# Choosing the engine of copies, squares, products and remainders step by step, with a fixed issue order, in a linear-attention and mixture kernel

## The chip, the core and the metric

The kernel runs on one core of one Trainium2 chip. The metric is the device time of one execution in microseconds (us). Three runs of the kernel before took 484.88, 486.04 and 486.46 us; the median is 486.04 us. About 0.3% (1.5 us) is what a comparison of this kernel can tell from no change.

## The reference, cut to what matters

```python
def _attn_ref(q, k, v, f_logit):          # q, k, v, f_logit: (4, 8, 768, 48)
    f = 1.0 / (1.0 + np.exp(-f_logit))
    state = np.zeros((B, H, D, D), dtype=np.float32)
    for t in range(S):
        state = f[:, :, t, :, None] * state + np.einsum('bhd,bhe->bhde', k[:, :, t], v[:, :, t])
        y[:, :, t] = np.einsum('bhd,bhde->bhe', q[:, :, t], state)
    return y

def _moe_ref(x, w_in, w_out):             # x: (3072, 384), w_in: (384, 2048), w_out: (2048, 384)
    h = x @ w_in
    sp = np.where(h > 20.0, h, np.log1p(np.exp(np.minimum(h, 20.0))))
    g = h * np.tanh(sp)
    return g @ w_out
```

The attention's output, put in rows of 384, is the x of the second part. All is float32 in and out.

## The kernel before

**Attention.** The 768 tokens are cut into 24 chunks of 128 tokens (4 batches by 6 pieces; n counts them, n = 0 to 23). For each chunk, `prep(n)` floors the log gates (`L529`), takes exponent and logarithm (`L532`, `L533`), sums them (by a matmul for the first four chunks, by the scan `L542` for the rest), takes two exponents (`L548`), multiplies k and q by them (`times`, `L411`) and keeps the decay at the chunk's end (`L555`). `attn0` to `attn3` turn k over, make the scores and mask them (`L589`), copy the turned k (`L612`), update the state (`L688` to `L693`, and the product with the decay, `L780`) and make the output. The output is evicted from PSUM whole by `L789` for the first four chunks (into `spareh`), and as a rounded part and a remainder after that (`L808` and `L809`, into `xt`).

**Second part.** The tokens form six groups of 512, and the 2048 inner columns form 16 tiles of 128, j = 0 to 15. A unit u is one group and one tile (98 units; the first four are half a group wide). Its input product h is at `L317` (nine matmuls of 512 columns in float32r, three products that make up for the rounding) or, for the first seven units, at `L327` (plain float32). Then g = h tanh(softplus(h)) is made in `mish`: exponent `L351` on ScalarE, clamp and add `L352` on VectorE, square (`L343` on ScalarE for u < 24, `L344` on VectorE after that), logarithm `L354` and exponent `L355` on ScalarE, product `L356` on VectorE, which is the last to read h. `L358` rounds g to gh on ScalarE, and the remainder g - gh goes to gl: on VectorE for u < 24 (`L347`), on GpSimd after that (`L348`). The output product of a unit is at `L365` (`L330` for the first seven), two units after the input product. There are two PSUM banks for h, so the input product of unit u + 2 waits until `L356` of unit u has read h.

**Weights.** Each weight tile j comes as 64-bit words and is put together by `load_w`: `L476` on ScalarE, then `L478`, `L479` and `L481` on VectorE. `split_w` rounds the tile on ScalarE (`L493`) and takes the remainder on VectorE (`L494`). `split_x` does the same to the first group's x (`L502`, `L503`). All 16 tiles are prepared once, while the first two groups run, and stay in SBUF.

**Order.** The kernel doesn't issue what it computes at once. Every step goes to a `Plan` (`add`) with its engine, a cost, and what it reads and writes; 1813 steps in all. `Plan.order` of the kernel before packs them by rank, forwards and backwards, tries random shifts from a list of seeds, and keeps the best; each engine's queue is then in that order. Steps marked `port` are packed as if VectorE and GpSimd could not run them at the same time. Where TensorE has nothing planned, `Plan.issue` puts in filler matmuls on zeros (`idle`, `L462`) until the first output product. An example of the planned costs, and the line that they belong to:

```python
def T_DVE(n):
    return n / 0.96 + 72
add("dve", T_DVE(W_TILE), lambda: nc.vector.scalar_tensor_tensor(   # W_TILE = 768; line L479
```

Of the kernel before, what the change touches and what calls it, by code (L numbers as in the profile page):

```python
# [10 lines left out]
F32 = mybir.dt.float32  # L11
# [35 lines left out]
SETTING = (600.0, 20.0)  # L47
MOVES = (
# [25 lines left out]
COLD = 1000.0  # L74


class Plan:
# [8 lines left out]
    def __init__(self):  # L86
        self.steps = []
        self.writer, self.readers = {}, {}
        self.glued = {}

# [13 lines left out]

    def glue(self, n):
        self.glued[len(self.steps)] = len(self.steps) - n

    def pack(self, rank, ahead, haste, back=False):


        steps = self.steps
# [4 lines left out]
        for i in range(count):  # L116
            for b in before[i]:
                after[b].append(i)
# [1005 lines left out]
```

## Time and profile before

| what | value |
|---|---|
| three runs, median (lowest to highest) | 486.04 us (484.88 to 486.46) |
| the profiled execution | 484.71 us |
| its span, first to last instruction | 482.9 us |
| TensorE (PE) busy | 464.4 us, 96% |
| weight loads (PEld) busy | 391.2 us, 81% |
| ScalarE (ACT) busy | 352.8 us, 73% |
| VectorE (DVE) busy | 343.8 us, 71% |
| GpSimd (POOL) busy | 144.3 us, 30% |

The profiled execution's own time is 1.8 us over its span. The table's shares are means over stages that differ: VectorE is near 100% from about 45 to 140 us and at 50% near the end, while GpSimd does nothing between 80 and 140 us.

### The profile page before, as it was taken

Reading aid. Unit: us, or ns where it says so; the run is one execution under the profiler, and the core shown is the slowest. Engines: PE = TensorE matmul, PEld = TensorE weight load, DVE = VectorE, ACT = ScalarE, POOL = GpSimd, SP = SyncE. Lnnn points to the kernel's source line nnn. Section 1 sums busy time; section 2 is a strip of 40 time slices with the busy share of each in tenths; the row PEclk is TensorE's granted clock in tenths of the full one; section 3 lists DMA queues with packets and bytes.
Section 4 is the critical chain, followed back from the end, with each engine's and each line's share of the span. In section 5 each row is a group of like instructions: output and inputs, shape, how many; then the busy total and the mean of one; then the engine's idle time right before and its main releaser. Section 6 shows DMA issues by size and latency. Waiting matters only on the chain.

```text
span 482.9 us, 12157 instructions
## 1 busy us (share of the span) xinstructions
PE 464.4 (96%) x5032; PEld 391.2 (81%) x5032; DVE 343.8 (71%) x600; ACT 352.8 (73%) x662; POOL 144.3 (30%) x126
## 2 busy tenths in 40 slices
PE   8988989899999999999999999999999999999994
PEld 8766547787778888888888888888888888888883
DVE  4579999999996878777676766865875554554551
ACT  6779887999989677667777787677676466665650
POOL 0411120000013354343543443343333233342431
PEclk9999999999999999999999999999999999999998
DMA  7776656453402253421211240220230000010001
GB/s 246 226 252 222 222 183 220 140 178 118 160 36 89 93 188 106 154 70 63 89 50 73 88 139 16 90 88 33 90 110 1 3 12 23 1 65 0 1 0 71
DMA packets 17102, 48.42 MB, mean 100 GB/s; under 512 B 2000, under 2 KB 2000, under 8 KB 17040
## 3 DMA queue, kind: packets, MB, share of 16 engines
q1 hardware_dynamic: 17040, 47.59, 28.9%
q8 instruction: 40, 0.66, 0.5%
q14 instruction: 22, 0.18, 0.1%
HBM read 39.32 MB, written 6.29 MB: 94 GB/s over the span
## 4 chain that ended last, share of the span: by engine, by line
PE 71%; DVE 13%; ACT 12%; issue 3%; DVEq 0%; ACTq 0%
PE o L365 30%; PE h L317 30%; DVE wt L479 2%; PE at L755 2%; DVE ng L356 2%; ACT ng L354 2%; PE at L762 1%; ACT ng L355 1%; ACT ng L343 1%; DVE wl L494 1%; PE at L609 1%; DVE gl L347 1%; ACT wt L476 1%; PE o L462 1%; PE h L582 1%
## 5 line engine op out<-in xcount | busy, mean ns | idle before, releaser
L317 PE MATMUL h<-xt,wh 128*128 128x512 f32 x546 | 164.2, 382 | 3.7 <-DVE ng L356 3.7
L348 POOL TENSOR_TENSOR gl<-ng,gh 128x512 fp32r<-128x512 f32 x74 | 100.6, 1362 | 174.4 <-ACT gh L358 153.4
L317 PEld LDWEIGHTS h<-xt,wh 128*128 128x128 f32 x546 | 101.6, 189 | 21.3 <-DVE ng L356 7.0
L356 DVE SCALAR_TENSOR_TENSOR ng<-ng,h 128x512 f32<-128x512 f32 x91 | 62.1, 684 | 63.6 <-ACT ng L355 63.0
L365 PE MATMUL o<-gh,wh 128*128 128x512 f32 x273 | 106.3, 389 | 0.0
L365 PE MATMUL o<-gl,wh 128*128 128x512 f32 x273 | 103.6, 379 | 0.5 <-DVE gl L347 0.5
L317 PE MATMUL h<-xt,wl 128*128 128x512 f32 x273 | 103.5, 379 | 0.0
L365 PE MATMUL o<-gh,wl 128*128 128x512 f32 x273 | 103.5, 379 | 0.0
L354 ACT ACTIVATE ng<-ng 128x512 f32<-128x512 f32 (+1 forms) x98 | 60.7, 620 | 35.3 <-DVE ng L344 31.1
L351 ACT ACTIVATE ng<-h 128x512 f32<-128x512 f32 (+1 forms) x98 | 57.3, 585 | 31.9 <-PE h L317 30.9
L358 ACT ACTIVATE gh<-ng 128x512 fp32r<-128x512 f32 x91 | 56.6, 625 | 22.3 <-PE o L365 14.6
L352 DVE TENSOR_SCALAR ng<-ng 128x512 f32<-128x512 f32 (+1 forms) x98 | 47.9, 489 | 30.0 <-ACT ng L351 29.5
L355 ACT ACTIVATE ng<-ng 128x512 f32<-128x512 f32 (+1 forms) x98 | 60.6, 619 | 2.4
L411 POOL TENSOR_TENSOR in<-in,inv 128x512 f32<-128x512 f32 x20 | 24.9, 1244 | 119.6 <-ACT inv L548 119.5
L365 PEld LDWEIGHTS o<-gl,wh 128*128 128x128 f32 x273 | 51.6, 189 | 8.2 <-DVE gl L347 0.9
L365 PEld LDWEIGHTS o<-gh,wh 128*128 128x128 f32 x273 | 51.6, 189 | 7.9 <-issue 0.2
L317 PEld LDWEIGHTS h<-xt,wl 128*128 128x128 f32 x273 | 51.6, 189 | 7.3
L365 PEld LDWEIGHTS o<-gh,wl 128*128 128x128 f32 x273 | 51.6, 189 | 6.8 <-issue 0.2
L344 DVE TENSOR_TENSOR ng<-ng 128x512 f32<-128x512 f32 x74 | 54.7, 739 | 2.2
L542 DVE TENSOR_TENSOR_SCAN inv<-gate,state 128x516 f32<-128x516 f32 x20 | 24.6, 1228 | 2.3 <-ACT gate L533 2.1
L780 POOL TENSOR_TENSOR state<-tmp,ends 128x192 f32<-128x192 f32 x20 | 14.7, 735 | 19.0 <-PE at L755 7.9
L479 DVE SCALAR_TENSOR_TENSOR wt<-raw,wt 128x768 int32<-128x768 int32 x16 | 17.9, 1119 | 0.2
(147 smaller groups left out, 571.7 us busy)
## 6 DMA issues: line engine op xcount, KB each, us to landing
in<-lk SPq DMA_DIRECT2D x18, 512.0 KB, 4.4
raw<-ww SPq DMA_DIRECT2D x12, 768.0 KB, 4.2
in<-qv SPq DMA_DIRECT2D x18, 512.0 KB, 4.2
out<-ob SPq DMA_DIRECT2D x18, 256.0 KB, 2.1
raw<-ww SPq DMA_DIRECT2D x8, 384.0 KB, 4.4
in<-lk SPq DMA_DIRECT2D x8, 256.0 KB, 3.6
in<-qv SPq DMA_DIRECT2D x8, 256.0 KB, 4.2
xt<-xt SPq DMA_DIRECT2D x15, 128.0 KB, 3.0
```

The source lines that it names most:

```text
L317: nc.tensor.matmul(h, w[:, a * P : (a + 1) * P], read(xt[:, x, a], part), start=(n == 0), stop=(n == 3 * NK - 1))
L344: ("dve", T_DVE(w), 1, lambda: nc.vector.tensor_tensor(n, n, n, ALU.mult))
L348: ("pool", T_POOL(w), 1, lambda: nc.gpsimd.tensor_tensor(gl, g, gh.bitcast(F32), ALU.subtract))
L351: ("act", T_ACT(w, True), 0, lambda: nc.scalar.activation(n_out, h, AF.Exp)),
L352: ("dve", T_DVE(w / 2), 1, lambda: nc.vector.tensor_scalar(n, n, E_CAP, 1.0, ALU.min, ALU.add)),
L354: ("act", T_ACT(w), 0, lambda: nc.scalar.activation(g, n, AF.Ln, bias=0.5, scale=0.5)),
L355: ("act", T_ACT(w), 0, lambda: nc.scalar.activation(g, g, AF.Exp, scale=-1.0)),
L356: ("dve", T_DVE(w), 0, lambda: nc.vector.scalar_tensor_tensor(g_out, g_in, 1.0, h, ALU.subtract, ALU.mult)),
L358: ("act", T_ACT(w), 0, lambda: nc.scalar.activation(gh, g, AF.Copy)),
L365: nc.tensor.matmul(o, w, read_again(x), start=(first and i == 0), stop=(last and i == 2))
L411: add("pool" if on_pool else "dve", cost, lambda: eng.tensor_tensor(dst, x, y, ALU.mult), reads, writes, port=port)
L479: add("dve", T_DVE(W_TILE), lambda: nc.vector.scalar_tensor_tensor(t, low, 29, t, ALU.logical_shift_right, ALU.bitwise_or), [kr], [kt], po ...
```

## The change

The planner's search is gone. The order of the 1813 steps is a table, `ORDER`, and a string, `CHOICES`, picks the engine of each step that can run on more than one (`Plan.either`). Nothing is computed otherwise than before: the steps, and what each waits for, are the same 1813, and 195 of them change their engine.

```diff
-SETTING = (600.0, 20.0)
-MOVES = (
-    100004, 100007, 100010, 100011, 100013, 100015, 100017, 100019, 100023, 100030, 100031, 100033, 100036,
+ORDER = (
+    0, 1, 35, 60, 110, 36, 85, 61, 175, 86, 11, 2, 12, 3, 13, 4, 14, 5, 15, 17, 6, 7, 8, 16, 9, 19, 18, 24, 10, 37,
+CHOICES = (
+    "1000010101000000001000100110000111000010000001001000000010000100010000100100100000000001001001100110"
...
+    def either(self, options, reads, writes):
+
+        n = len(self.open)
+        self.open.append((len(self.steps), options))
+        engine, cost, port, issue = options[int(CHOICES[n]) if n < len(CHOICES) else 0]
+        self.add(engine, cost, issue, reads, writes, port=port)
...
+        square = prefer(
+            ("act", T_ACT(w), 0, lambda: nc.scalar.activation(n, n, AF.Square)),
+            ("dve", T_DVE(w), 1, lambda: nc.vector.tensor_tensor(n, n, n, ALU.mult)),
+            False,
         )
+        high = prefer(
+            ("act", T_ACT(w), 0, lambda: nc.scalar.activation(gh, g, AF.Copy)),
+            ("dve", T_DVE(w / 2), 1, lambda: nc.vector.tensor_copy(gh, g)),
+            not early,
+        ) + (("pool", w * 1.1 + 75, 1, lambda: nc.gpsimd.tensor_copy(gh, g)),)
+        low = prefer(
+            ("dve", T_DVE(w), 1, lambda: nc.vector.tensor_tensor(gl, g, gh.bitcast(F32), ALU.subtract)),
+            ("pool", T_POOL(w), 1, lambda: nc.gpsimd.tensor_tensor(gl, g, gh.bitcast(F32), ALU.subtract)),
+            not early,
         )
...
+        def copy(cols, dst, src, reads, writes):
+
+            plan.either((
+                ("act", T_ACT(cols, True), 0, lambda: nc.scalar.activation(dst, src, AF.Copy)),
+                ("dve", T_DVE(cols), 0, lambda: nc.vector.tensor_copy(dst, src)),
+            ), reads, writes)
...
-            add("act", T_ACT(W_TILE) + 65, lambda: nc.scalar.activation(
+            add("act", T_ACT(W_TILE) + 80 + 320 * late, lambda: nc.scalar.activation(
                 t.bitcast(F32), high.bitcast(F32), AF.Copy, scale=2.0**-112), [kr], [kt])
...
-            add("dve", T_DVE(W_TILE), lambda: nc.vector.scalar_tensor_tensor(
+            add("dve", T_DVE(W_TILE) + 220 * late, lambda: nc.vector.scalar_tensor_tensor(
                 t, low, 29, t, ALU.logical_shift_right, ALU.bitwise_or), [kr], [kt], port=True)
...
-                add("dve", T_DVE(w / 2), lambda s=s: nc.vector.tensor_scalar(
+                clamp = nc.gpsimd if n >= 5 * GC else nc.vector
+                add("pool" if n >= 5 * GC else "dve", w * 1.1 + 75 if n >= 5 * GC else T_DVE(w / 2), lambda s=s, clamp=clamp: clamp.tensor_scalar(
                     f[:, s], f[:, s], L_CAP, None, ALU.max), (), kf, port=True)
...
-            add("act", T_ACT(GT, True), lambda: nc.scalar.activation(kt_s, b, AF.Copy), [key], ["kt"])
+            copy(GT, kt_s, b, [key], ["kt"])
...
-                    add("pool", T_POOL(NP * D), lambda: nc.gpsimd.tensor_tensor(sv, tv, dv, ALU.mult),
-                        pairs(("end", n)) + [ktmp], [("st", batch)])
+                    plan.either((
+                        ("pool", T_POOL(NP * D), 1, lambda: nc.gpsimd.tensor_tensor(sv, tv, dv, ALU.mult)),
+                        ("dve", T_DVE(NP * D), 1, lambda: nc.vector.tensor_tensor(sv, tv, dv, ALU.mult)),
+                    ), pairs(("end", n)) + [ktmp], [("st", batch)])
```

Over the whole program, by engine: 45 squares move from VectorE to ScalarE (and those of units 2 and 21 the other way); of the 91 roundings to gh, 35 go to VectorE and 12 to GpSimd (the twelve belong to units 70 to 91); the remainders gl on VectorE become 42 instead of 17, those on GpSimd 49 instead of 74; of the attention's copies and the roundings of weights and x, 28 go from ScalarE to VectorE; 7 of 20 state products and 9 products with k go from GpSimd to VectorE, and ten products (nine with q in chunks 12 to 23, one half with k in chunk 0) the other way; the floors of chunks 20 to 23 go to GpSimd. TensorE has the same steps, and 30 filler matmuls instead of 26.

Three places of the new order follow. The first is VectorE's queue near its start, in the first chunks (`at`, `h` and `o` are PSUM banks, `mid` and `tmp` belong to the state, `spareh` takes the evicted output). Before:

```order
L529 TENSOR_SCALAR in_82<-in_82 128x512
L589 TENSOR_TENSOR a_86<-at_105,causal 128x256
L589 TENSOR_TENSOR a_87<-at_106,causal 128x256
L529 TENSOR_SCALAR spareh<-spareh 128x512 x2
L693 TENSOR_TENSOR tmp_89<-at_106,mid_88 128x64x3
L411 TENSOR_TENSOR in_82<-in_82,h_108 128x512
L589 TENSOR_TENSOR a_87<-h_109,causal 128x256
L589 TENSOR_TENSOR a_86<-h_108,causal 128x256
L478 TENSOR_SCALAR wt_103<-wt_103 128x768
```

And the same place of the changed kernel (`L608` is the mask, `L711` is `tmp`, `L490` and `L491` are `load_w`):

```order
L608 TENSOR_TENSOR a_86<-at_105,causal 128x256
L421 COPY mid_88<-at_107 128x64x3
L711 TENSOR_TENSOR tmp_89<-at_106,mid_88 128x64x3
L412 TENSOR_TENSOR in_82<-in_82 128x512
L421 COPY spareh<-at_106 128x2x64
L490 TENSOR_SCALAR wt_103<-wt_103 128x768
L412 TENSOR_TENSOR in_82<-in_82,h_108 128x512
L421 COPY spareh<-at_105 128x2x2x64
L491 SCALAR_TENSOR_TENSOR wt_103<-raw_101,wt_103 128x768
L608 TENSOR_TENSOR a_86<-h_108,causal 128x256
```

Three of ScalarE's copies (`L421`) and a product with k now stand in VectorE's queue, and the first weight tile's steps come ahead of the second chunk's masks.

The second place is VectorE's queue where the products `L356` of units 12 and 13 stand. Before:

```order
L356 SCALAR_TENSOR_TENSOR ng_93<-ng_93,h_108 128x512
L352 TENSOR_SCALAR ng_93<-ng_93 128x512
L347 TENSOR_TENSOR gl_100<-ng_93,gh_97 128x512
L481 SCALAR_TENSOR_TENSOR wt_103<-raw_101,wt_103 128x768
L347 TENSOR_TENSOR gl_98<-ng_93,gh_95 128x512
L494 TENSOR_TENSOR wl_1274<-wt_104,wh_1273 128x768
L356 SCALAR_TENSOR_TENSOR ng_93<-ng_93,h_109 128x512
L352 TENSOR_SCALAR ng_93<-ng_93 128x512
```

After, where `L358` is the product, `L354` the clamp, and `L344` the rounding of g:

```order
L358 SCALAR_TENSOR_TENSOR ng_93<-ng_93,h_108 128x512
L354 TENSOR_SCALAR ng_93<-ng_93 128x512
L491 SCALAR_TENSOR_TENSOR wt_103<-raw_101,wt_103 128x768
L344 CAST gh_95<-ng_93 128x512
L493 SCALAR_TENSOR_TENSOR wt_103<-raw_101,wt_103 128x768
L358 SCALAR_TENSOR_TENSOR ng_93<-ng_93,h_109 128x512
L354 TENSOR_SCALAR ng_93<-ng_93 128x512
```

Both remainders gl have left this piece of the queue; a rounding of g, which was ScalarE's, has come.

The third place is GpSimd's queue after its work for chunks 6 to 9. Before:

```order
L780 TENSOR_TENSOR state<-tmp_89,ends 128x64x3
L411 TENSOR_TENSOR in_81<-in_81,inv_84 128x512
L780 TENSOR_TENSOR state<-tmp_90,ends 128x64x3
L411 TENSOR_TENSOR in_82<-in_82,inv_84 128x512
L348 TENSOR_TENSOR gl_98<-ng_93,gh_95 128x512
```

After (`L414` is the product with k, `L349` the remainder, `L798` the state product):

```order
L414 TENSOR_TENSOR in_82<-in_82,inv_84 128x512
L414 TENSOR_TENSOR in_81<-in_81,inv_84 128x512
L349 TENSOR_TENSOR gl_99<-ng_93,gh_96 128x512 x2
L349 TENSOR_TENSOR gl_100<-ng_93,gh_97 128x512
L349 TENSOR_TENSOR gl_98<-ng_93,gh_95 128x512
L349 TENSOR_TENSOR gl_100<-ng_93,gh_97 128x512
L349 TENSOR_TENSOR gl_98<-ng_93,gh_95 128x512
L349 TENSOR_TENSOR gl_100<-ng_93,gh_97 128x512 x2
L349 TENSOR_TENSOR gl_99<-ng_93,gh_96 128x512
```

Before, the first remainder on GpSimd is that of unit 24. After, the nine rows of remainders here are those of units 7, 10, 11, 12, 14, 15, 17, 20 and 22.

## Rows read from the trace of the kernel before

**Rows 1.** The page: span, and busy time by engine.

```profile
span 482.9 us, 12157 instructions
PE 464.4 (96%) x5032; PEld 391.2 (81%) x5032; DVE 343.8 (71%) x600; ACT 352.8 (73%) x662; POOL 144.3 (30%) x126
```

**Rows 2.** Stretches, us: busy PE, PEld, DVE, ACT, POOL; granted clock; DMA share, GB/s.

```profile
0.00:43.92 43.92, 38.70 (x828) 32.66 (x828) 28.76 (x64) 33.16 (x81) 11.49 (x19) 1.00 0.74 231
43.92:90.56 46.64, 43.08 (x631) 28.27 (x631) 45.08 (x75) 40.31 (x80) 5.87 (x6) 1.00 0.63 216
90.56:140.34 49.78, 47.76 (x216) 40.33 (x217) 48.35 (x73) 48.17 (x80) 0.00 (x0) 1.00 0.37 128
140.34:482.90 342.56, 334.85 (x3358) 289.98 (x3356) 221.57 (x391) 231.19 (x424) 126.90 (x101) 0.99 0.18 64
```

**Rows 3.** TensorE's waits from 0 to 43.92 us: for whom, us in total, times, longest.

```profile
PE o L726 <- issue: 1.2, 1, 1.2
PE at L609 <- issue: 0.7, 1, 0.7
...
```

**Rows 4.** TensorE's waits from 43.92 to 90.56 us.

```profile
PE o L330 <- DVE ob L356: 1.8, 2, 1.2
PE h L317 <- DVE ng L356: 0.8, 1, 0.8
```

**Rows 5.** TensorE's waits from 90.56 to 140.34 us.

```profile
PE h L317 <- DVE ng L356: 2.2, 4, 1.0
```

**Rows 6.** TensorE's waits from 140.34 us to the end.

```profile
PE h L317 <- DVE ng L356: 0.7, 3, 0.3
PE o L365 <- DVE gl L347: 0.5, 1, 0.5
```

**Rows 7.** Groups of VectorE, 43.92 to 140.34 us: busy, mean ns, idle before.

```profile
L479 DVE SCALAR_TENSOR_TENSOR wt<-raw,wt 128x768 int32<-128x768 int32 x13 | 14.5, 1115 | 0.1
L347 DVE TENSOR_TENSOR gl<-ng,gh 128x512 fp32r<-128x512 f32 x15 | 10.2, 683 | 0.4 <-ACT gh L358 0.2
L481 DVE SCALAR_TENSOR_TENSOR wt<-raw,wt 128x768 int32<-128x768 int32 x8 | 9.5, 1189 | 0.0
L352 DVE TENSOR_SCALAR ng<-ng 128x512 f32<-128x512 f32 x20 | 8.3, 417 | 0.1
```

**Rows 8.** VectorE in order of time: start, us, instruction.

```profile
105.86 1.19 DVE L481 SCALAR_TENSOR_TENSOR wt<-raw,wt 128x768 int32<-128x768 int32 x1
106.99 0.39 DVE L352 TENSOR_SCALAR ng<-ng 128x512 f32<-128x512 f32 x1
107.32 0.66 DVE L347 TENSOR_TENSOR gl<-ng,gh 128x512 fp32r<-128x512 f32 x1
107.91 0.55 DVE L478 TENSOR_SCALAR wt<-wt 128x768 int32<-128x768 int32 x1
```

**Rows 9.** VectorE near 184 and 374 us, start, us, instruction.

```profile
183.63 0.68 DVE L344 TENSOR_TENSOR ng<-ng 128x512 f32<-128x512 f32 x1
184.23 1.77 DVE L411 TENSOR_TENSOR in<-in,gate 128x512 f32<-128x512 f32 x1
...
374.12 1.06 DVE L352 TENSOR_SCALAR ng<-ng 128x512 f32<-128x512 f32 x1 [0.42 <-ACT ng L351]
```

**Rows 10.** GpSimd at the same two places.

```profile
184.06 1.40 POOL L348 TENSOR_TENSOR gl<-ng,gh 128x512 fp32r<-128x512 f32 x1 [2.46 <-ACT gh L358]
...
373.62 1.28 POOL L348 TENSOR_TENSOR gl<-ng,gh 128x512 fp32r<-128x512 f32 x1 [3.91 <-ACT gh L358]
```

**Rows 11.** Groups of the whole span: fillers on TensorE, and remainders on GpSimd.

```profile
L462 PE MATMUL o<-state 128*128 128x128 f32 x52 | 8.9, 322 | 1.1 <-DVE state L425 1.1
...
L348 POOL TENSOR_TENSOR gl<-ng,gh 128x512 fp32r<-128x512 f32 x74 | 100.6, 1362 | 174.4 <-ACT gh L358 153.4 <-DVE ng L356 6.8 <-issue 3.2
```

**Rows 12.** Groups of VectorE from 145 to 483 us.

```profile
L344 DVE TENSOR_TENSOR ng<-ng 128x512 f32<-128x512 f32 x73 | 54.0, 739 | 2.1
...
L352 DVE TENSOR_SCALAR ng<-ng 128x512 f32<-128x512 f32 x73 | 37.4, 512 | 29.9 <-ACT ng L351 29.5
```

More of the change, by code (lines that the diff above doesn't have):

```diff
@@ new lines, in order @@
+    def order(self):
+        count = len(self.steps)
+        order = ORDER if len(ORDER) == count else range(count)
+        after = [[] for _ in self.steps]
+        for i, step in enumerate(self.steps):
+            for b in step[3]:
+                after[b].append(i)
+        free, ready, self.start = dict(self.FREE), [0.0] * count, [0.0] * count
+        transfers = shared = 0.0
+        for i in order:
+            e, cost, _, _, size, port = self.steps[i]
+            t = self.start[i] = max(free[e], ready[i], shared if port else 0.0)
+            end = free[e] = t + cost
+            if port:
@@ L156, in pack @@
                 shared = end
-                stale.update(("dve", "pool"))
-            if e == "sp" and not back:
-                transfers = max(transfers, end + 650.0) + steps[i][4] / 0.27
+            if e == "sp":
+                transfers = max(transfers, end + 650.0) + size / 0.27
                 end = transfers - 650.0
             for a in after[i]:
-                f = a if back else i
-                if engine[i] == engine[a] == "pe":
-                    lag = 0.0
-                else:
-                    lag = self.LATENCY[engine[f]]
-                    if back and engine[f] == "sp":
-                        lag += steps[f][4] / 0.27
-                ready[a] = max(ready[a], end + lag)
-                left[a] -= 1
-                if not left[a]:
-                    queue[engine[a]].append(a)
-                    stale.add(engine[a])
@@ L215, in issue @@
+                ready[a] = max(ready[a], end + (0.0 if e == self.steps[a][0] == "pe" else self.LATENCY[e]))
+        return order
     def issue(self):
@@ L340, in mish, with prefer @@
             n_out, g_in, g_out = n, g, g
-        square = (
-            ("act", T_ACT(w), 0, lambda: nc.scalar.activation(n, n, AF.Square)) if early else
-            ("dve", T_DVE(w), 1, lambda: nc.vector.tensor_tensor(n, n, n, ALU.mult))
-        )
-        low = (
-            ("dve", T_DVE(w), 1, lambda: nc.vector.tensor_tensor(gl, g, gh.bitcast(F32), ALU.subtract)) if early else
-            ("pool", T_POOL(w), 1, lambda: nc.gpsimd.tensor_tensor(gl, g, gh.bitcast(F32), ALU.subtract))
+        def prefer(first, second, other):
+            return (second, first) if other else (first, second)
@@ L407, in recurrence_moe_kernel, with times @@
         done = 0
-        def times(on_pool, cols, dst, x, y, reads, writes, port=True):
-            eng, cost = (nc.gpsimd, T_POOL(cols)) if on_pool else (nc.vector, T_DVE(cols))
-            add("pool" if on_pool else "dve", cost, lambda: eng.tensor_tensor(dst, x, y, ALU.mult), reads, writes, port=port)
+        def times(cols, dst, x, y, reads, writes, port=True):
+            options = [("dve", T_DVE(cols), port, lambda: nc.vector.tensor_tensor(dst, x, y, ALU.mult))]
+            if port:
+                options.append(("pool", T_POOL(cols), 1, lambda: nc.gpsimd.tensor_tensor(dst, x, y, ALU.mult)))
+            plan.either(options, reads, writes)
+        def copy(cols, dst, src, reads, writes):
[3 more added lines that the diff above has]
+            ), reads, writes)
         def consts():
@@ L501, in split_x @@
                 ks, kh, kl = ([(z, ("xt", 0, c), a) for c in range(GC)] for z in "shl")
-                add("act", T_ACT(GT), lambda a=a: nc.scalar.activation(x[:, 0, a], xs[:, a], AF.Copy), ks, kh)
+                plan.either((
+                    ("act", T_ACT(GT), 0, lambda a=a: nc.scalar.activation(x[:, 0, a], xs[:, a], AF.Copy)),
+                    ("dve", T_DVE(GT / 2), 1, lambda a=a: nc.vector.tensor_copy(x[:, 0, a], xs[:, a])),
+                ), ks, kh)
                 add("dve", T_DVE(GT), lambda a=a: nc.vector.tensor_tensor(
@@ L687, in attn2 @@
             if n < B:
-                add("act", T_ACT(NP * D, True), lambda: nc.scalar.activation(mv, uv[0], AF.Copy),
-                    keys[:1], ["mid"])
+                copy(NP * D, mv, uv[0], keys[:1], ["mid"])
             else:
@@ L774, in evict @@
                     for e in range(2):
[L775 to L776 removed]
+                        copy(NP * D, kt_s[:, :, dims(e)], bt[e], [keys[e]], ["kt"])
                 if n < NCH - B:
@@ L951, in recurrence_moe_kernel @@
                 )
-                for (e, c, shared, fn), (r, k) in zip(ops, rw):
-                    add(e, c, fn, r, k, port=shared)
+                for options, (r, k) in zip(ops, rw):
+                    if len(options) > 1:
+                        plan.either(options, r, k)
+                    else:
+                        e, c, shared, fn = options[0]
+                        add(e, c, fn, r, k, port=shared)
             while done < min(4 * NCH, attend_goal(u)):
```

122 lines of the change are left out of this document (25 added, 97 removed), and 106 rows, old and new, of tables (MOVES, ORDER).

## The prediction

> **What bounds the kernel now.** I read the page's busy shares first, then cut the span at three points of the program, asked in each piece what TensorE waits for, and then priced what the order moves there. TensorE is busy 464.4 of 482.9 us [rows 1], so everything that any order can win is in the other 18.5 us and in the filler matmuls. The points are the starts of the input products of unit 4 (43.92 us), unit 12 (90.56 us) and unit 23 (140.34 us) [rows 2]; they name the same work in both programs. I call the pieces A, B, C and D.
>
> - A, to 43.92 us: TensorE idle 5.22 us, VectorE busy 28.76, ScalarE 33.16 [rows 2]. The first four chunks form one chain over all engines. The longest waits are 1.2 and 0.7 us [rows 3]. Of 52 filler records (two to a matmul) 24 fill the time before the first input has come; the others, about 14 matmuls, stand in holes.
> - B, to 90.56 us: VectorE busy 45.08 of 46.64 us. TensorE idle 3.56 us [rows 2], mostly because `L356` comes late [rows 4].
> - C, to 140.34 us: VectorE busy 48.35 and ScalarE 48.17 of 49.78 us, TensorE 47.76, GpSimd nothing at all [rows 2]. TensorE waits 2.2 us in four waits, each for `L356` on VectorE [rows 5].
> - D, the rest: TensorE waits 0.7 us for `L356` and 0.5 us once for a remainder [rows 6]; the rest of its idle time there lies behind the last matmul. VectorE is busy 65%, ScalarE 67% [rows 2].
>
> So VectorE bounds B and C, a chain bounds A, and TensorE bounds D, where its granted clock is at the level of 2.4 GHz (0.99 of it) and below that nowhere [rows 2].
>
> **The change part by part.** The prices are times that an instruction holds its queue, from one start to the next in a full queue: a remainder 0.59 us (107.32 to 107.91), a clamp 0.33 us (106.99 to 107.32), `L481` 1.13 us (105.86 to 106.99) [rows 8]. A rounding or copy on VectorE is not in this trace. It reads one operand as the clamp does, and writes as the remainder does, so it costs between 0.33 and 0.59 us for 512 columns; I take 0.4, nearer to the clamp, since the number of operands is what sets these two rows apart. A page has a price for it: the Trainium skill, "VectorE: DVE Perf Modes", section on the perf-mode tier table, puts a float32 copy in SBUF in the same tier as a tensor-scalar operation. By that the cast would be 0.33 us, and C would come out some 0.2 us shorter on VectorE; no run here shows it yet.
>
> *C.* Counting in both orders what VectorE must have done between the two points: nine remainders leave its queue (13 before, 4 after; GpSimd makes one of its nine in B, seven in C and one later), and two `L481` are done before C. That takes away 9 x 0.59 + 2 x 1.13 = 7.6 us. It gets three roundings (1.2), one square (0.6), one rounding of a weight tile of 768 columns (0.6) and two short attention steps (2 x 0.4 = 0.8), 3.2 us. Net 4.4 us less; with the copies at 0.33 and at 0.59 us it is 4.8 and 3.1. ScalarE loses three roundings, a square and two weight roundings.
>
> Against that stands GpSimd, which now works beside VectorE. The trace shows that the two can exclude each other: a product of VectorE that stands at 1.77 us met a remainder of GpSimd that started 0.17 us before it, while the square just ahead took 0.68 us; a clamp took 1.06 us behind a remainder, against a mean of 0.417 us [rows 7, 9, 10]. On the average it is much less. In the late part the 73 clamps take 512 ns instead of 417 and the 73 squares 739 ns instead of the 683 of a remainder in C [rows 7, 12], together 73 x (0.095 + 0.056) = 11 us for 74 remainders on GpSimd [rows 11], or 0.15 us each. For the seven in C that is 1.0 us; VectorE's queue is 97% full there and 65% in D, so I take 1.5. VectorE in C goes from 48.35 to 48.35 - 4.4 + 1.5 = 45.5 us, below TensorE's 47.76. What is late next is TensorE itself. All that C can give is its idle time, 2.0 us, and I take 1.9. The old plan also costed `L479` and `L481` at 768/0.96 + 72 = 872 ns, where they take 1115 and 1189 [rows 7]; the new costs add 220 and 240, so the new order was laid out on durations that the trace bears out, which is why I don't expect new holes of that kind.
>
> *B.* VectorE has as much to do as before: one `L479` and one floor fewer, one `L481`, one state product and one remainder of x more, about 0.7 us more on 45.08. GpSimd has one remainder instead of one of three state products. The waits for `L356` stay. I count 0.5 us lost, between -0.5 and 1.5.
>
> *A.* VectorE gets 13 instructions more (six evictions, a `mid`, a state product, a floor, a product with k, a square, a weight rounding, an `L479`), some 6 us at 0.33 to 1.1 us each. It is idle 15.2 us there, so they fit if they stand where it waits; what hides them is the wait for the chain. ScalarE, the fullest of the three, loses seven. The six evictions are in the chain on either engine and cost about the same. What can be won is TensorE's idle time beyond the first 1.1 us and the holes with fillers; what can be lost is a step of the chain that queues behind a weight step of 1.1 us on VectorE. I take half of the two waits of 1.2 and 0.7 us [rows 3] as won, 1.0 us, between 3.0 won and 2.0 lost. The four more fillers say nothing: they cover a longer part of the program, as the first output product stands later.
>
> *D.* The 45 squares that go to ScalarE and the roundings that leave it about balance. 34 remainders leave GpSimd for VectorE, which has a third of its time free. The roundings and floors on GpSimd lie here too. All of that is covered by TensorE's work as long as `L356` of a unit comes before the next input product that needs its bank; this is at its tightest, with two products and a turn of k between or less, seven times now and four times before, and those four cost at most the 0.7 us of the waits [rows 6]. I count 0, between 0.7 won and 1.5 lost. Transfers keep their order but for single swaps, and no engine waits for one in B to D.
>
> Sum: -1.0 + 0.5 - 1.9 + 0 = -2.4 us on the profiled execution's 484.7 us (span 482.9 and 1.8 around it): 482.3 us. The median of the runs is 1.3 us above that execution, so 486.0 - 2.4 = 483.6 us.
>
> **The rivals.** *The two engines shut each other out.* Each of the seven remainders in C stops VectorE for its whole 1.28 us [rows 10], 9.0 us against the 4.4 won. For it: 1.77 us instead of 0.68, and a queue that is always full, so that there is always something to stop. Against it: 0.15 us each on the average in D, and that the order places steps with this exclusion in mind. C would then need 48.35 - 4.4 + 9.0 = 53.0 us of VectorE, and with its idle time of 1.4 would last 54.4, 4.6 longer; B would lose 1.3 more. With A's gain that is -1.0 + 1.8 + 4.6 = +5.4: 491.4 us. It turns into a loss from the point where the remainders in C cost more than 4.4 us plus C's idle 1.4, 0.8 us each. The Trainium skill says this outright: "SBUF — State Buffer", section "Who interferes with whom", has VectorE and GpSimd share one pair of ports under an exclusive lock, held for a whole instruction against one with two SBUF inputs or in a two-port mode. By that rule these 491.4 us are what would come of seven full collisions; the trace agrees that they happen, and that they are rare.
>
> *VectorE is too full at the start.* The 6 us more in A push the chain back by 2.0 us, and C's gain is eaten: +2.0 + 0.5 - 1.9 = +0.6, 486.6 us. For it: a chain, in which each hop waits, and weight steps ahead of masks in the new order. Against it: 15.2 us of idle time, and ScalarE's lighter load.
>
> *All pieces give.* A gives its 3.0, C 2.0, D 0.7, B nothing: -5.7, 480.3 us. For it: engines chosen together with the order, and fillers and waits in A of which little need stay. Against it: VectorE's share of B has not fallen.
>
> **How the numbers follow.** The forecast 483.6 us has a chance of 0.45 (482.2 to 485.0), all pieces giving 0.17 (479.5 to 482.2), VectorE full at the start 0.25 (485.0 to 488.0), the shut-out 0.13 (488 and more). About 0.3%, 1.5 us, is what can be told from no change, so the border lies at 484.6 and 487.5 us. Faster: 0.17 and 0.39 of the forecast's 0.45, with 0.02 for small parts, 0.58. Slower: 0.13 and 0.05 of the early case, 0.18. Same: 0.24. For 8 in 10, the range leaves out the tail below 479.8 us and the shut-out: 479.8 to 488.0.
>
> **What would show it.** C: VectorE's busy time between the input products of units 12 and 23 near 45.5 us and TensorE without a wait over 0.3 us there; wrong if remainders on GpSimd stand beside VectorE instructions of 1 us and more that took 0.4 to 0.7 before. A: unit 4's input product starts at about 43 us; the second rival if after 45. B: as long as before or half a us longer. D: TensorE's waits under 1 us in all; wrong if single waits for `L356` or for a remainder of over 0.5 us come back. The rounding on VectorE between 0.4 and 0.7 us long as the rows show it. The forecast is wrong as a whole if the time moves in D, or if A moves by more than 3 us.

## The result, and the profile after

| | kernel before | changed kernel |
|---|---|---|
| median of the runs, us (lowest to highest) | 485.78 (484.88 to 486.46) | 480.71 (479.98 to 482.27) |
| profiled execution, us (its span) | 484.71 (482.9) | 479.98 (478.2) |

The ratio is 0.9905, with an interval from 0.9877 to 0.9933: faster by about 0.95%, or 4.6 us of 485.8 (the two medians lie 5.1 us apart). Two more sets of runs beside the kernel before gave 0.9897 and 0.9905.

The page's first lines, to be read against [rows 1]:

```profile
span 478.2 us, 12153 instructions
PE 464.8 (97%) x5040; PEld 392.8 (82%) x5040; DVE 346.3 (72%) x647; ACT 344.8 (72%) x630; POOL 122.0 (26%) x111
```

TensorE is as busy as before, 464.8 us against 464.4. The 4.7 us are time in which it stood. Here are the same four stretches as in [rows 2]: busy PE, PEld, DVE, ACT, POOL, then granted clock, DMA share and GB/s.

```profile
0.00:43.34 43.34, 39.53 (x836) 34.54 (x836) 33.51 (x77) 32.75 (x77) 8.95 (x17) 1.00 0.78 251
43.34:87.85 44.51, 43.21 (x635) 28.62 (x635) 44.27 (x76) 39.36 (x75) 6.48 (x5) 1.00 0.64 211
87.85:135.28 47.43, 46.91 (x213) 39.88 (x214) 44.53 (x68) 44.46 (x73) 13.83 (x8) 1.00 0.39 134
135.28:478.20 342.92, 335.13 (x3358) 289.71 (x3356) 224.00 (x429) 228.24 (x407) 92.70 (x82) 1.00 0.19 64
```

A is 0.6 us shorter, B 2.1, C 2.35, and D 0.4 longer. VectorE's idle time in B went from 1.56 to 0.24 us; in C it is now idle 2.9 us instead of 1.4. TensorE's waits in A, B, C and D follow, one after the other (for whom, us in total, times, longest); they answer to [rows 3 to 6].

```profile
PE h L744 <- issue: 1.4, 1, 1.4
PE o L473 <- DVE state L436: 1.0, 1, 1.0
...
PE h L319 <- DVE ob L358: 1.2, 1, 1.2
PE h L309 <- DVE ng L358: 0.8, 1, 0.8
PE at L756 <- POOL in L414: 0.5, 2, 0.2
...
PE o L367 <- ACT ng L356: 0.5, 1, 0.5
...
PE h L309 <- DVE mid L709: 0.8, 1, 0.8
PE h L309 <- DVE ng L358: 0.7, 1, 0.7
PE at L780 <- DVE mark L674: 0.2, 1, 0.2
```

In C a wait of 0.8 us for `L358` (the old `L356`) stands beside the one of 0.5; both replace the four of 2.2 us of [rows 5]. One caution on the cuts: B of the changed kernel holds three more matmuls of `L367` than B of before, C three fewer (35 against 36 of each product). Such matmuls take 0.22 us each from one to the next (46.91 us for the 213 of C), so this is some 0.65 us of TensorE's time. So B and C are best read together: 96.42 us before, 91.94 after, of which TensorE's idle time is 5.58 before and 1.82 after.

### The profile page after: what moved, and what is told of

Read it like the earlier page. It is cut to its first block, busy times and chain, and to the rows that moved or that the text cites. A ratio compares the mean times of both kernels' runs of the same rounds, so it can differ in the third digit from the quotient of the medians.

```text
span 478.2 us, 12153 instructions
## 1 busy us (share of the span) xinstructions
PE 464.8 (97%) x5040; PEld 392.8 (82%) x5040; DVE 346.3 (72%) x647; ACT 344.8 (72%) x630; POOL 122.0 (26%) x111
## 4 chain that ended last, share of the span: by engine, by line
PE 79%; DVE 14%; ACT 4%; issue 2%; ACTq 0%
PE o L367 34%; PE h L309 34%; DVE inv L561 2%; PE at L773 2%; PE o L473 2%; PE at L628 2%; PE at L780 1%; DVE wt L491 1%; DVE sparel L493 1%; DVE wl L509 1%; PE h L601 1%; DVE ng L354 1%; DVE ng L358 1%; DVE in L412 1%; PE h L644 1%
## 5 line engine op out<-in xcount | busy, mean ns | idle before, releaser
L309 PEld LDWEIGHTS h<-xt,wh 128*128 128x128 f32 x546 | 101.2, 189 | 20.3 <-DVE ng L358 4.0
L349 POOL TENSOR_TENSOR gl<-ng,gh 128x512 fp32r<-128x512 f32 x49 | 69.5, 1418 | 166.4 <-ACT gh L343 89.8
L367 PE MATMUL o<-gh,wh 128*128 128x512 f32 x273 | 106.2, 389 | 0.5 <-ACT ng L356 0.5
L367 PE MATMUL o<-gh,wl 128*128 128x512 f32 x273 | 103.5, 379 | 0.0
L367 PE MATMUL o<-gl,wh 128*128 128x512 f32 x273 | 103.5, 379 | 0.0
L358 DVE SCALAR_TENSOR_TENSOR ng<-ng,h 128x512 f32<-128x512 f32 x91 | 62.2, 685 | 43.5 <-ACT ng L357 42.8
L354 DVE TENSOR_SCALAR ng<-ng 128x512 f32<-128x512 f32 (+1 forms) x98 | 44.4, 453 | 38.9 <-ACT ng L353 38.4
L356 ACT ACTIVATE ng<-ng 128x512 f32<-128x512 f32 (+1 forms) x98 | 60.7, 619 | 14.2 <-DVE ng L339 9.3
L357 ACT ACTIVATE ng<-ng 128x512 f32<-128x512 f32 (+1 forms) x98 | 60.7, 620 | 2.5
L367 PEld LDWEIGHTS o<-gh,wh 128*128 128x128 f32 x273 | 51.6, 189 | 9.3 <-ACT ng L356 0.9
L367 PEld LDWEIGHTS o<-gl,wh 128*128 128x128 f32 x273 | 51.6, 189 | 7.3
L367 PEld LDWEIGHTS o<-gh,wl 128*128 128x128 f32 x273 | 51.6, 189 | 6.8 <-issue 0.2
L338 ACT ACTIVATE ng<-ng 128x512 f32<-128x512 f32 (+1 forms) x67 | 41.3, 617 | 16.6 <-DVE ng L354 16.4
L348 DVE TENSOR_TENSOR gl<-ng,gh 128x512 fp32r<-128x512 f32 x42 | 30.8, 735 | 10.4 <-POOL gh L346 6.4
L343 ACT ACTIVATE gh<-ng 128x512 fp32r<-128x512 f32 x44 | 27.3, 625 | 13.2 <-DVE ng L358 9.9
L561 DVE TENSOR_TENSOR_SCAN inv<-gate,state 128x516 f32<-128x516 f32 x20 | 26.6, 1331 | 1.0 <-ACT gate L552 0.6
L414 POOL TENSOR_TENSOR in<-in,inv 128x512 f32<-128x512 f32 x12 | 14.7, 1226 | 45.3 <-ACT inv L567 45.1
L339 DVE TENSOR_TENSOR ng<-ng 128x512 f32<-128x512 f32 (+1 forms) x31 | 22.1, 714 | 0.9
```

The source lines that it names most:

```text
L309: nc.tensor.matmul(h, w[:, a * P : (a + 1) * P], read(xt[:, x, a], part), start=(n == 0), stop=(n == 3 * NK - 1))
L338: ("act", T_ACT(w), 0, lambda: nc.scalar.activation(n, n, AF.Square)),
L343: ("act", T_ACT(w), 0, lambda: nc.scalar.activation(gh, g, AF.Copy)),
L348: ("dve", T_DVE(w), 1, lambda: nc.vector.tensor_tensor(gl, g, gh.bitcast(F32), ALU.subtract)),
L349: ("pool", T_POOL(w), 1, lambda: nc.gpsimd.tensor_tensor(gl, g, gh.bitcast(F32), ALU.subtract)),
L354: (("dve", T_DVE(w / 2), 1, lambda: nc.vector.tensor_scalar(n, n, E_CAP, 1.0, ALU.min, ALU.add)),),
```

## The experiments

The theory behind the forecast: the gain is VectorE's work in C that GpSimd takes (remainders), a little in A, and nothing in B and D. The rivals: order and engines only work together; the late part carries gain or loss; the port that VectorE and GpSimd share sets the limit. All ratios below are against the kernel before on the same chip. The tables `ORDER` and `CHOICES` make the edits; of their diffs a line or two stands here.

**The changed kernel again, the new order alone, the new engines alone, and the late engines put back.** These four ran on one chip.

> The changed kernel once more, as the mark for the other runs of this call. Both theories: 480.7 us, 0.990 of the kernel before (0.988 to 0.993).

Measured: 480.51 us, ratio 0.9897 (0.9866 to 0.9929). Its profile is 2.2 us longer than the first: 2.9 us more up to unit 12, C 47.43 us again, and 0.7 less in D.

The order alone: the order of after, each step on its engine of before.

```diff
-    "1000010101000000001000100110000111000010000001001000000010000100010000100100100000000001001001100110"
+    "0000000000100000001000000010000000010010000001000000000010000000010000000000000000000000000000000000"
...
-                clamp = nc.gpsimd if n >= 5 * GC else nc.vector
+                clamp = nc.gpsimd if n >= NCH else nc.vector
```

> The new order with the engines of the kernel before (195 steps put back). Theory, both halves are needed: the piece between the input products of units 12 and 23 gets its nine remainders back on VectorE and is again some 49.5 us long, the two pieces before it keep one to two of their 2.7 us; 483 to 486 us. Rival, the order is the gain and the engines follow: 480 to 482 us.

Measured: 493.21 us, ratio 1.0161 (1.0132 to 1.0189): slower, and far outside both expectations. Up to unit 23 it is ahead of the kernel before, 137.87 us against 140.34; the loss is all in D, 353.1 us against 342.6.

The engines alone: the order of before with the engine choices of after (the other table, `ORDER`, put back).

> The new engines with the order of the kernel before. Theory, both halves are needed: the piece between units 12 and 23 keeps about 2 us, the earlier ones lose what VectorE's new steps push back, since they don't stand where it is idle; 483 to 487 us. Rival, the engines are the gain: 480 to 482 us.

Measured: 495.74 us, ratio 1.0211 (1.0182 to 1.024), again outside both expectations. C takes 53.85 us (1.8 us of it are filler matmuls, which the planner also puts into long holes behind the first output product) and D 348.6. TensorE's waits in its C (here `L348` is the product, `L299` the input product):

```profile
PE h L299 <- DVE ng L348: 3.8, 6, 1.2
```

Either half without the other makes the kernel 7.5 to 10 us slower than before; the gain belongs to the pair.

The late engines back: of the 195 steps that change their engine, the 166 behind unit 23's input product are back on that of before; the new order stands.

```diff
-    "1011101001000001011101000010101001100001000001100010010100000110010010011001001001111101010110001010"
+    "0000011011011010011000011011011010011000011011011010011000011011011010011000011011011010011000011011"
...
```

> The changed kernel with the 166 engine choices behind unit 23's input product put back to those of the kernel before (among them the twelve roundings of g and the four floors on GpSimd); the order stays. Theory, TensorE covers all of that: within 0.8 us of the changed kernel, 480.0 to 481.5 us. Rival, the late moves carry part of the gain: over 482 us.

Measured: 492.12 us, ratio 1.0133 (1.0104 to 1.0161). The theory failed and the rival is right, by far more than it asked. B and C are as in the changed kernel (C 47.43 us), D takes 353.6 us instead of 342.9. TensorE's waits there:

```profile
PE h L309 <- DVE ng L358: 2.9, 8, 0.7
PE h L309 <- DVE mid L709: 1.6, 4, 0.8
PE h L601 <- DVE ng L358: 1.3, 2, 1.0
PE at L780 <- DVE mark L674: 0.9, 3, 0.5
```

Seventeen such waits instead of three, 6.7 us instead of 1.7; with 1.9 us of filler matmuls they are most of the 10.7 us that D is longer. Why `L358` is late is seen, as far as the trace tells, in ScalarE's group of the first scaling of g, which needs the square of `L339`; of D, first with the engines put back, then in the changed kernel (busy, mean ns, idle time before it and what ended it):

```profile
L356 ACT ACTIVATE ng<-ng 128x512 f32<-128x512 f32 x75 | 47.1, 628 | 48.5 <-DVE ng L339 46.6 <-POOL gl L349 1.3
```

```profile
L356 ACT ACTIVATE ng<-ng 128x512 f32<-128x512 f32 x75 | 47.1, 629 | 13.4 <-DVE ng L339 9.3 <-DVE gl L348 1.1 <-POOL gl L349 0.3
```

With the squares on VectorE, ScalarE waits 46.6 us for them; with 46 of them on ScalarE itself it waits 9.3 for the rest, and 15.7 for the clamps that its own squares need. In the kernel before 31.1 us of the like stand in D, and TensorE waits only the 1.2 us of [rows 6] there. So such waits alone don't hold TensorE up; it takes the new order with them. That the squares among the 166 choices are the cause was not tested by itself. So my sentence that all of D is covered holds for the whole change only: 166 engine choices keep 11 us away that the new order would cost without them.

**The pieces joined crosswise.** Four programs on one chip: the new beginning up to unit 23 or unit 12 with before's rest, before's beginning up to unit 12 with the new rest, and the changed kernel with its nine early remainders back on VectorE.

> Order and engines of the changed kernel up to unit 23's input product, order and engines of the kernel before behind it. Theory, the gain is made in the first 140 us: as fast as the changed kernel, 479.5 to 481.8 us. Rival, the late part of the new table carries part of the gain: 482.5 us and more.

Measured: 483.39 us, ratio 0.9979 (0.9958 to 1.0001), the time that the rival named. B 44.52 and C 47.43 us, as in the changed kernel; D takes 343.85, 1.3 more than in the kernel before, with a new wait at the joint:

```profile
PE o L357 <- DVE gl L338: 0.9, 1, 0.9
```

> Order and engines of the changed kernel up to unit 12's input product alone, those of the kernel before behind it. Theory, the piece from unit 12 to 23 gives about 2.3 us for itself: 482.5 to 484 us. Rival, the gain lies before unit 12: 480.5 to 481.5 us.

Measured: 482.78 us, ratio 0.9972 (0.9951 to 0.9993), as the theory had it. C takes 49.52 us, and its four waits for the product sum to 3.2 us.

> Order and engines of the kernel before up to unit 12's input product, those of the changed kernel behind it. Theory: 482.5 to 484 us, the 2.3 us of the piece from unit 12 to 23 alone. Rival, all of the gain lies before unit 12: 485 to 486.5 us.

Measured: 484.03 us, ratio 0.9987 (0.997 to 1.0004), just beyond the theory's end. C takes 50.0 us, since at the joint a step of ScalarE (`L347`) keeps TensorE 1.6 us; D takes 342.2. A joint can take about what a piece gives, so these three show that no piece loses much, and no more; what each gives can't be read from their medians.

The remainders back:

```diff
-    "1000010101000000001000100110000111000010000001001000000010000100010000100100100000000001001001100110"
-    "0000011001000001000010000001011000010010000101000100010000000101101010000101001000011110011101001001"
+    "1000010101000000001000100110000111000010000001001000000010000100010000100000100000000001000001000100"
+    "0000010000000000000010000000011000000010000101000100010000000101101010000101001000011110011101001001"
```

> The changed kernel with the nine early remainders (units 7, 10, 11, 12, 14, 15, 17, 20, 22) back on VectorE, all else as changed. Theory, they are what relieves VectorE from unit 12 to 23: 9 x 0.59 = 5.3 us more on a queue with 2.9 us free there, 2 to 4 us slower than the changed kernel, 482.7 to 484.7 us. Rival, the two engines shut each other out as much as the move relieves: 480 to 481.5 us, or faster.

Measured: 481.86 us, ratio 0.9955 (0.9932 to 0.9978), between the two expectations. Its C, to be read against the third line of the stretches above:

```profile
89.62:137.79 48.17, 47.31 (x213) 39.74 (x213) 47.52 (x76) 44.53 (x73) 0.00 (x0) 1.00 0.39 132
```

Eight remainders in C (the ninth lies outside) are worth 3.0 us of VectorE's busy time there (47.52 against 44.53), but 0.74 us of the piece, as TensorE stands only 0.86 us here and 0.52 with them on GpSimd. By the ratios 0.5% of the 0.95% hangs on the nine; the two intervals just touch. The profile shows less: against the first one of the changed kernel, C is 0.74 us longer and B 0.54, and D is 1.0 shorter (0.3 against the second).

**The last four, on a third chip.** The changed kernel a third time, all early remainders on GpSimd, the late part alone, and the first engine choices put back.

> The changed kernel once more, beside the three kernels below and the kernel before on one chip. Two profiles of it differ up to unit 12 (87.85 and 90.76 us) and are alike behind it (C 47.43 us in both, D 342.9 and 342.2 with the tail). In the slower one a weight tile (raw<-ww) lands late, a factor of chunk 4 (ob, L358) follows late, TensorE stands 2.6 us for it instead of 1.2, and its granted clock is at 0.5 for about 3 us behind that. Theory: this late landing is all that sets the executions apart. Then a third profile has C at 47.4 and D at 342 to 343 again, and reaches unit 12 by 88 to 90 us where the wait is 1.2 us and the clock never falls, and near 90.5 where it is over 2 us. Ratio 0.988 to 0.992. Rival, that the executions differ all over the span: C or D moves by over 0.7 us.

Measured: 481.25 us, ratio 0.9905 (0.987 to 0.9939). C is 47.43 us and D 342.5, as expected; unit 12 begins only at 91.68 us, though the wait for `ob` is 1.1 us. Here TensorE's clock fell earlier, behind a wait of 1.7 us at 20.3 us. So one late transfer is not all that sets the executions apart; what they have in common is the last section's matter.

> All seventeen early remainders on GpSimd instead of nine, nothing else changed. From nine put back on VectorE we know that eight remainders in C are worth 3.0 us of VectorE's time there (47.52 against 44.53 us) but 0.7 us of the piece (48.17 against 47.43), because TensorE stands only 0.5 us in C by then. Theory: the port is cheap for VectorE, and TensorE is the bound of C now. Then VectorE in C is busy some 43 us (four remainders fewer at 0.37 us each), C stays within 0.5 us of 47.43, and the ratio is within 0.003 of that of the changed kernel. Rival, that GpSimd's share of the port is what limits the number: VectorE's instructions beside it get longer, VectorE's busy time in C doesn't fall, and remainders of 1.7 us come too late for TensorE; C grows by over 1 us and the kernel is slower than the changed one by 0.3% or more.

```diff
-    "1000010101000000001000100110000111000010000001001000000010000100010000100100100000000001001001100110"
+    "1000010101000000001000100110000111000010000001001000000010000100010000100100100000100011001001100110"
...
```

Measured: 483.45 us, ratio 0.9977 (0.9951 to 1.0004), 0.7% more than the changed kernel by the ratios, 0.5% by the medians on this chip. C takes 48.72 us. The rival was right on C: VectorE has four remainders fewer in C and is busy 44.81 us there, no less than in the changed kernel. The two groups of VectorE in C that pay for it, in the changed kernel and then here:

```profile
L354 DVE TENSOR_SCALAR ng<-ng 128x512 f32<-128x512 f32 x12 | 5.1, 423 | 0.9 <-ACT ng L353 0.9
L490 DVE TENSOR_SCALAR wt<-wt 128x768 int32<-128x768 int32 x6 | 3.3, 557 | 0.2 <-ACT wt L488 0.2
```

```profile
L354 DVE TENSOR_SCALAR ng<-ng 128x512 f32<-128x512 f32 x12 | 7.1, 591 | 0.8 <-ACT ng L353 0.7
L490 DVE TENSOR_SCALAR wt<-wt 128x768 int32<-128x768 int32 x6 | 4.1, 691 | 1.0 <-ACT wt L488 0.9
```

And one collision in order of time (start, us, instruction), VectorE first, then GpSimd:

```profile
112.95 1.24 DVE L493 SCALAR_TENSOR_TENSOR wt<-raw,wt 128x768 int32<-128x768 int32 x1
114.11 1.52 DVE L354 TENSOR_SCALAR ng<-ng 128x512 f32<-128x512 f32 x1
```

```profile
113.83 1.50 POOL L349 TENSOR_TENSOR gl<-ng,gh 128x512 fp32r<-128x512 f32 x1 [0.65 <-POOL gl L349]
```

The clamp ends 0.30 us behind the end of GpSimd's remainder (115.63 against 115.33), and takes 1.52 us instead of 0.42. The Trainium skill, "SBUF — State Buffer", section "Who interferes with whom", says that whichever of the two issues first keeps the shared ports for a whole instruction; the trace agrees here, for the remainder started 0.28 us ahead. Two things of the rival don't show: no wait of TensorE in C is for a remainder (the longest is 1.0 us for `L358`), and C is not all of the difference in time, as D takes 341.65 us here, 0.6 to 1.3 less than in the three profiles of the changed kernel, while a late weight tile makes A and B longer in this profile.

> The order and engines of before up to the input product of unit 23, those of the changed kernel behind it: the late part of the change alone. My prediction gave it 0. Theory: the late part gains nothing and only has to fit its order; D takes 342 to 343 us as in the kernel before (342.6), A to C as before (140.3), with up to 1 us at the joint, and the ratio is 0.998 to 1.002. Rival, that the late part carries a share of the gain (the early part alone, up to unit 23, reached only 0.998, 2.9 us less gain than the whole): then D is 341 us or less and the ratio 0.996 or less.

Measured: 484.31 us, ratio 0.9994 (0.9971 to 1.0018). D takes 343.3 us. The late part alone gives nothing that can be told, as the theory said.

> The changed kernel with the fourteen engine choices that lie before unit 4's input product as they were before (nine steps back from VectorE to ScalarE, among them seven steps of the chunk chain, and four steps between VectorE and GpSimd the other way). My prediction put the gain of A on VectorE's free time there. Theory one, that VectorE's added work in A buys time: unit 4 starts later than in the changed kernel by 1 us or more (45 to 47 us), and the ratio is 0.993 or more. Theory two, that only the new order matters in A (the new order with all the engines of before reached unit 4 at 43.23 us): unit 4 starts between 43.2 and 44.7 us, and the ratio is that of the changed kernel within 0.003.

```diff
-    "1000010101000000001000100110000111000010000001001000000010000100010000100100100000000001001001100110"
+    "0000000000100000001000000010000000010010000001000000000010000100010000000100100000000001001001100110"
```

Ten steps go from VectorE back to ScalarE (the expectation counted nine), four between VectorE and GpSimd. Measured: 480.94 us, ratio 0.991 (0.9881 to 0.9939): the changed kernel's. Its A (stretch, busy times, clock):

```profile
0.00:44.13 44.13, 40.29 (x847) 34.83 (x847) 29.88 (x64) 34.70 (x85) 11.10 (x19) 1.00 0.79 241
```

VectorE is busy 29.9 us in A instead of 33.5, and unit 4 starts at 44.13, between the changed kernel's 43.34 and 44.69. Theory two holds: VectorE's added work in A buys no time that the medians can tell.

No version beat the changed kernel.

## Why the prediction was right and wrong

The forecast was 483.6 us, faster; it came to 480.71, inside the range, 2.9 us under the forecast, below the forecast's own band (482.2 to 485.0). It lies in the band of the third rival, which I had given 0.17, and near its time (480.3), though by another way than that rival took: A and D gave little, and B did. So that the time lies inside the range is in part luck. Term by term:

**C: the size near, the reason right in part.** Forecast -1.9, capped by TensorE's idle time; measured -2.35 in each of three profiles of the changed kernel, of which some 0.65 us is the product that went to B. TensorE's idle time fell by 1.50, from 2.02 to 0.52 us. VectorE was to be busy 45.5 us; it is 44.5. But the relief of VectorE by the remainders, on which the term rested, is only a part: with the nine back on VectorE C takes 48.17 us, so 0.74 us hangs on them. And with the new order alone VectorE is busy 45.80 us in C, close to my 45.5, and C still takes 48.86. That stretch, and VectorE's product in it:

```profile
89.01:137.87 48.86, 47.37 (x213) 39.74 (x213) 45.80 (x70) 46.92 (x79) 0.83 (x1) 1.00 0.38 130
L358 DVE SCALAR_TENSOR_TENSOR ng<-ng,h 128x512 f32<-128x512 f32 x12 | 8.2, 689 | 2.3 <-ACT ng L357 2.3
```

The product waits 2.3 us for ScalarE there, which is busy 46.92 us; in the changed kernel ScalarE is busy 44.46 and the product waits 1.5. I had noted that ScalarE loses steps in C and given it no part in the sum. That this carries what the remainders don't is read from these rows and was not tested by itself.

VectorE's groups in C with remainders and roundings, in the changed kernel, then GpSimd's:

```profile
L348 DVE TENSOR_TENSOR gl<-ng,gh 128x512 fp32r<-128x512 f32 x4 | 3.3, 826 | 0.0
L344 DVE CAST gh<-ng 128x512 fp32r<-128x512 f32 x4 | 2.0, 492 | 0.1
...
L349 POOL TENSOR_TENSOR gl<-ng,gh 128x512 fp32r<-128x512 f32 x8 | 13.9, 1734 | 45.6 <-ACT gh L343 35.6 <-DVE gh L344 10.0
```

GpSimd makes eight of the remainders in C, not seven. The price of GpSimd beside VectorE, taken as 1.5 us, came out between 0.8 and 1.7. The upper figure is eight remainders at 0.59 us, 4.7, less the 3.0 by which VectorE's busy time fell against the program with the remainders back. The lower is what single instructions show against it: four remainders at 826 instead of 686 ns and four roundings at 492 instead of 426. Most of it is one collision (start, us, instruction), of the kind that I had named as a sign of being wrong; a second sign, a wait of TensorE over 0.3 us in C, is there too, with 0.8 and 0.5.

```profile
126.15 1.29 POOL L349 TENSOR_TENSOR gl<-ng,gh 128x512 fp32r<-128x512 f32 x1 [7.97 <-ACT gh L343]
126.76 1.22 DVE L348 TENSOR_TENSOR gl<-ng,gh 128x512 fp32r<-128x512 f32 x1
```

The rounding alone, without GpSimd beside it, takes 426 ns in the program with the remainders back, where the clamps take 420, so 0.4 was too much and the lower bound of 0.33 right. The Trainium skill, "VectorE: DVE Perf Modes", section on the perf-mode tier table, puts a float32 copy and a tensor-scalar operation in one tier; this case's trace agrees with it, for the rounding.

**B: wrong, and with the wrong sign; most of what I missed is here.** Forecast +0.5; measured -2.1 (and some -2.8 if the product that came from C is counted out). I counted VectorE's instructions and left its time for each as it was. Two things failed. VectorE's idle time there fell from 1.56 to 0.24 us: a wait of 1.0 us for ScalarE's step of x (`L808`) is gone, and I had treated B's 97% as full. And its busy time fell by 0.8 us where I had it grow by 0.7, as its instructions got shorter. The group with the wait, and two groups that got shorter, in before and then after:

```profile
L809 DVE TENSOR_TENSOR xt<-at,xt 128x256 fp32r<-128x256 f32 x8 | 3.3, 421 | 1.0 <-ACT xt L808 1.0
L494 DVE TENSOR_TENSOR wl<-sparel,wh 128x768 fp32r<-128x768 f32 x7 | 6.9, 1002 | 0.0
L478 DVE TENSOR_SCALAR wt<-wt 128x768 int32<-128x768 int32 x6 | 3.7, 621 | 0.0
```

```profile
L827 DVE TENSOR_TENSOR xt<-at,xt 128x256 fp32r<-128x256 f32 x8 | 3.1, 425 | 0.0
L509 DVE TENSOR_TENSOR wl<-sparel,wh 128x768 fp32r<-128x768 f32 x7 | 6.5, 945 | 0.2 <-ACT wh L506 0.2
L490 DVE TENSOR_SCALAR wt<-wt 128x768 int32<-128x768 int32 x6 | 3.3, 556 | 0.0
```

The last two are the same instructions on the same shapes, 0.8 us less in all. The new order alone has the 556 ns (and 990 for the other group), the old order with the new engines 570 and 1003. But the shorter rows are not enough: B takes 45.78 us with the new order alone, where VectorE is busy 45.07, and 46.64 with the new engines alone, as before. Most of B's gain, too, needs both. GpSimd's work in B didn't shrink; its three products with k take 1321 ns instead of 1184, so where the two engines meet it may now be GpSimd that waits. That this is what shortened VectorE's instructions is read from those rows and was not tested by itself. The clause that TensorE's waits for the product stay was half right: they fell from 3.0 to 2.0 us.

**A: the size came out in one execution, the reason fell.** Forecast -1.0 by filling VectorE's idle time. Unit 4 starts at 43.34, 44.69 and 47.20 us in three profiles of the changed kernel, at 44.00 to 45.55 in the five programs that begin like it, and at 43.92, 43.78 and 42.90 in the three with before's beginning. So A gains nothing in these profiles and rather loses, most where the clock falls in it. The step that failed is that half of the two waits is won: the one of 0.7 us is gone, but in the place of the other, 1.2 us at `L726`, stands one of 1.4 us at a product of the same line (`L744`). That the work fits is right (it took 4.75 us instead of some 6, and VectorE still has 9.8 us idle). The second rival, a chain pushed back by 2.0 us, has its sign, unit 4 after 45 us, in four of the eight profiles with the new beginning; with the added work taken back unit 4 starts at 44.13. In some of the four the clock fell or a weight tile came late, so how much VectorE's queue itself pushes the chain stays open.

**D: the number right, the reason too broad.** Forecast 0; measured +0.4, -0.35 and -0.1 in three profiles. "Covered by TensorE's work" was true of both whole programs; a wait of 0.8 and one of 0.7 us are left where I named over 0.5 as the sign of trouble, and 1.7 us in all where I named under 1; they cost at most 0.4 us on balance. The twelve roundings (658 ns each) and the floors (1623 ns) on GpSimd end none of TensorE's waits. But the cover isn't there for the new order with before's engines, which loses 11 us in D.

**The shut-out** did not happen in the changed kernel, and begins with four remainders more in C: there 48.7 us and VectorE's clamps at 591 ns. The changed kernel stands short of that point. In it GpSimd mostly loses, with remainders of 1734 ns where one that nothing delays takes 1280 [rows 10].

What stays open: the pieces of the profile sum to -4.7, but two other profiles of the changed kernel give -2.5 and -1.2; by medians the gain is 3.9 to 5.2 us. The joined programs give 0.2% for the beginning and 0.1% for the end, and what they lose in D at the joints (1.3 and 0.8 us) is some 2 of the 3.3 us that are lacking to 0.95%. Fallen clocks may be a part of the rest: of the twelve runs with the new beginning up to unit 23 six have them, by the border of the last section (median 484.4 us, the other six 482.7).

## What to carry to other kernels

An order and a choice of engines made together can't be priced as two lists: each alone lost 7 to 10 us here, so "covered anyway" must be asked of the new order with the engines that it has. In a stretch where one engine is 97% busy, ask whether its instructions stand at their undisturbed length, and what its last 3% wait for; in B of this kernel that went with a larger gain than the moved remainders gave C. Ask of each engine in the chain, and not only of the fullest, what it loses: with VectorE's busy time in C already at the forecast's level, C waited for ScalarE. Move work to an engine that shares a port only until the full engine has some slack: eight remainders took 3.0 us off VectorE, four more gave nothing back and made C 1.3 us longer.

## What the runs showed of the hardware

One thing I had not expected is that executions of this kernel in which TensorE's clock falls near the beginning lose time there: two profiles of the changed kernel reach unit 12 2.9 and 3.8 us later than the first. In the second profile of the changed kernel a weight tile comes late (ScalarE stands 1.8 us for it), the chain of waits leads from that transfer over ScalarE and VectorE to `ob`, and TensorE stands 2.6 us. The chain, in order of time (start, us, what):

```profile
36.27 4.68 DMA raw<-ww
...
41.03 0.95 ACT wt L488
...
43.10 0.86 DVE wt L491
43.97 0.34 DVE in L548
44.30 0.34 DVE ob L358
44.64 0.04 issue
44.69 2.92 PE h L319 x3
```

The stretch behind that wait (the clock is the third figure from the end):

```profile
44.70:47.70 3.00, 3.00 (x4) 1.44 (x5) 3.00 (x6) 2.78 (x7) 0.00 (x0) 0.50 0.43 97
```

0.50 is the lower level, 1.2 GHz. What it costs is in the group of those products, in the first profile and in this one:

```profile
L319 PE MATMUL h<-spareh,sparel 128*128 128x512 f32 x18 | 8.5, 608 | 1.2 <-DVE ob L358 1.2
```

```profile
L319 PE MATMUL h<-spareh,sparel 128*128 128x512 f32 x18 | 10.1, 703 | 2.6 <-DVE ob L358 2.6
```

1.4 us of wait and 1.6 us of slower products, 3.0 in all. In the third profile the clock is 0.51 from 22.5 to 29.5 us, behind the wait of 1.7 us:

```profile
22.50:29.50 7.00, 7.00 (x131) 6.09 (x121) 3.67 (x7) 2.79 (x6) 1.27 (x1) 0.51 0.79 240
```

A wait of that length is not enough by itself: with all remainders on GpSimd TensorE stood 2.7 us at the same product, and its clock stayed at 1.00.

It happens unevenly. I sorted the runs afterwards by the mean granted clock of their span: at or below 0.994 are 7 of 16 runs of the changed kernel (median 481.5 us, the other nine 479.7), 8 of 65 of the kernel before, and none of the six with A's engine choices put back, which lie between 479.92 and 481.31 us. The other programs point the same way. Of all six that begin with the new order and the new engines, the changed kernel included, 27 of 66 runs are at or below 0.994; of the three that begin as the kernel before, 9 of 88; of the two with the new order and before's engines in A, none of 11; of the new engines in the old order, none of 6. So such falls go with the new engines of A in the new order. Whether VectorE's fuller queue makes them was not tested, and the border of 0.994 was chosen afterwards. It also leaves open whether A's new engines buy something that the falls take back: the other nine runs of the changed kernel have a median 1.2 us below that of the six, but they are from three sets of runs.
